# Last stage of a fused attention and two-layer kernel: each tile's eight transposes made together in two row halves, and the splits of the weight sums regrouped by inner block

## The chip, the core and the metric

The kernel runs on one core of a Trainium2 chip. The metric is the device time of one execution in microseconds (us). Smaller is better. TensorE (PE) multiplies and transposes; its weight loads are listed apart as PEld. VectorE (DVE), ScalarE (ACT) and GpSimd (POOL) do the elementwise work, and SyncE (SP) issues the DMAs. Every engine runs its own instructions in the order in which they stand.

## The reference

A causal attention, and behind it two feed-forward layers, the second with a SoLU and a layer normalisation between its two products. The change lies in the very last product, `ln @ w_out`, and in what feeds it.

```python
attn_out = causal_softmax(q @ k.T / 8) @ v        # 2 x 12 heads, 448 x 64
x = attn_out, heads side by side                  # 896 tokens x 768
h = x @ moe_w_in                                  # 768 x 2048
x = (h * sigmoid(h)) @ moe_w_out                  # 2048 x 768
h = x @ moe2_w_in                                 # 768 x 1024
e = np.exp(h - h_max)
sm = e / (np.sum(e, axis=-1, keepdims=True) + 1e-09)
solu = h * sm
mu = np.mean(solu, axis=-1, keepdims=True)
var = np.mean((solu - mu) ** 2, axis=-1, keepdims=True)
ln = (solu - mu) / np.sqrt(var + 1e-06) * g_ln
return (ln @ moe2_w_out).astype(np.float32)       # 1024 x 768
```

Products run in a reduced float32 format, so each operand is split into a high and a low part, and a product is three matmuls: high by high, high by low, low by high.

## The kernel before

The kernel goes through stages: attention, first layer up, first layer down, then the second layer. In the second layer the 896 tokens are seven tiles t = 0 to 6 of 128 rows. `gemm3(t)` (L647 to L649) makes the 128 x 1024 block of h in one of two tiles of the PSUM pool `psh` (two banks each). `chain(t)` turns it into ln: a maximum on DVE (L661), Exp on ACT (L662), scaling on DVE (L664 to L667), a Square on ACT that writes back into the `psh` tile (L669), and Identity on ACT (L670). The result stands in SBUF as `es4[t]`, eight blocks of 128 columns.

For the last product ln must be transposed. `turn(t, n)` (L680) transposes half a tile, four blocks of 128 x 128, into one bank of the pool `pst`, which has two buffers of one bank. `take(t, n)` then makes the two parts: ACT copies the bank into the high part (L684), DVE subtracts that from the bank into the low part (L685). `take` of both halves is the step `takes` for tile 1 and `take(0, 1)`, `take(0, 2)` for tile 0.

Tiles 0, 1 and 2 are multiplied plainly: `whole(t, n)` makes 24 matmuls for each half of the columns (`product`, L703 to L705) in one bank, and ACT scales the result to SBUF (L729). Tiles 3 to 6 go in two pairs by a Strassen-like scheme, `pair4(g)`: seven products of 12 matmuls, named after their operands ("11", "12", "s4", "s2", "s3", "s1", "22"), on sums of the transposed halves (made by `pre(g, n)`: L845, L691, L684, L685) and on weights or sums of weight blocks. DVE adds the results up (L743). The weight sums are made in place by `sums4(k)` for each inner block k = 0 to 3 (ACT scales four blocks, L825; POOL adds, L827 to L830). `split_t(z)` splits a weight sum t1 to t4 into parts, one copy on ACT (L836) and one subtraction on DVE (L837) for each k.

The order is written out by hand. `after()` is called behind each product, and the table `steps` says which of these preparations stand behind which call: call 0 and 1 belong to `whole(0, 0)`, 2 and 3 to `whole(0, 1)`, and so on to 11; calls 12 to 18 belong to `pair4(1)` and 19 to 25 to `pair4(2)`. `whole(0, 0)` itself is called inside `chain(6)`, between the scaling and the Square. In PSUM the seven tiles leave this division: two banks `gm` for the products, two `pst`, four `psh`; `psh` is given back behind `whole(2, 1)`, and `psq` (two banks for products) takes part of its place.

Of the kernel before, what the change touches and what calls it, by code (L numbers as in the profile page):

```python
# [80 lines left out]
def fused(ctx, tc, qk, vv, w1, w2, w3, w4, gl, out):  # L81
# [34 lines left out]
    with tc.manual_schedule():  # L116
# [514 lines left out]
        psd.release()  # L631
        pst = pool("pst", 2, space=PS)
        psh = pool("psh", 2, space=PS)
# [42 lines left out]

        def turn(t, n):
            tp = tps[t, n] = pst.tile([128, K2, 128], F32, name="tp", tag="tp")
            for m in range(K2):
                nc.tensor.transpose(tp[:, m], half(t, n - 1)[:, m], ident)  # L680

        def parts(z, x, low):
            h, l = aop[z]
            nc.scalar.activation(h, x, AF.Copy)  # L684
            low.tensor_tensor(l, x, h.bitcast(F32), ALU.subtract)  # L685

        def take(t, n, z=None):
            parts(z or (t, n), tps.pop((t, n)) if z is None else tps[t, n], nc.vector)

# [93 lines left out]
        for t in range(NT):  # L783
            gemm3(t)
            if t == 0:
                fill()
            if t == NT - 2:
                turn(0, 1)
                turn(0, 2)

            def first():
                if t == NT - 2:
                    take(0, 1)
                    take(0, 2)
                fill()

            if t < NT - 1:
                chain(t, first, fill)
# [10 lines left out]
        def arrive(t):  # L809
            turn(t, 1)  # L810
            turn(t, 2)
            take(t, 1)
            take(t, 2)
# [17 lines left out]

        def split_t(z, ks=range(K2)):
            q = {"t1": "11", "t2": "22", "t3": "12", "t4": "21"}[z]
            h, l = split[4, z]
            for k in ks:
                nc.scalar.activation(h[:, k], quads[q, k], AF.Copy)  # L836
                nc.vector.tensor_tensor(l[:, k], quads[q, k], h[:, k].bitcast(F32), ALU.subtract)  # L837

        def pre(g, n):
            a, b = 2 * g + 1, 2 * g + 2  # L840
            s1, s3, s2, s4 = half(b, 1), half(b, 0), half(a, 0), half(a, 1)
            if n == 0:
                turn(b, 1)
                turn(b, 2)
                nc.scalar.activation(s3, tps[b, 1], AF.Copy)  # L845
                add(s1, tps[b, 2], s3, ALU.add)
                take(b, 2, (g, "22"))
            elif n == 1:
                turn(a, 1)
                take(a, 1, (g, "11"))  # L850
                add(s2, s1, tps[a, 1], ALU.subtract)
                add(s3, s3, tps[a, 1], ALU.subtract)
            elif n == 2:
                turn(a, 2)
                take(a, 2, (g, "12"))
                add(s4, tps[a, 2], s2, ALU.subtract)
                parts((g, "s4"), s4, nc.gpsimd)
            else:
                z = ("s2", "s3", "s1")[n - 3]
                parts((g, z), {"s1": s1, "s2": s2, "s3": s3}[z], nc.gpsimd)  # L860

        steps = {1: [lambda: sums4(1)], 3: [lambda: sums4(2)], 4: [lambda: arrive(2)], 5: [lambda: sums4(3)],
                 6: [lambda: pre(1, 0)], 7: [lambda: pre(1, 1)], 8: [lambda: split_t("t2", (0, 1))],
                 9: [lambda: pre(1, 2)], 10: [lambda: split_t("t2", (2, 3))], 11: [lambda: pre(1, 3), lambda: split_t("t3")],
                 12: [lambda: split_t("t1"), lambda: pre(1, 4)], 13: [lambda: split_t("t4"), lambda: pre(1, 5)],
                 14: [lambda: pre(2, 0)], 15: [lambda: pre(2, 1)], 16: [lambda: pre(2, 2)],
# [11 lines left out]
        sums4(0)  # L878
        turn(1, 1)
        turn(1, 2)  # L880
        chain(NT - 1, takes, lambda: whole(0, 0))
        whole(0, 1)
        for t in (1, 2):
            for n in range(2):
                whole(t, n)
        psh.release()
        banks[0] = pool("psq", 2, space=PS)
        for g in (1, 2):
            pair4(g)
        banks = [q for q in banks if q is not gm]  # L890
        banks[0].release()
        pst.release()
# [54 lines left out]
```

## Time and profile before

| | |
|---|---|
| Median of three runs | 408.0 us (407.79 to 408.76) |
| The profiled execution, its own time | 408.79 us |
| Its span, first to last instruction | 407.0 us |
| PE busy in the span | 398.4 us (98%) |
| Chain of work that ended last, by engine | PE 85%, DVE 9%, ACT 4%, issue 1% |

How to read it: the profile lists one execution, each instruction with start and duration in us from the span's start. In a timeline, the brackets at a row's end give the engine's idle time just before it and the instruction whose end released it. Matmuls overlap: each starts when its predecessor is about half done. The share of busy time is a mean over stages; what counts for this change is the stretch from 335 us to the end.

### The profile page before, as it was taken

The page shows a single profiled execution, that of the slowest core. Times are in us where ns is not written, and L with a number is a line of the kernel's source. Part 1 is how long each engine was busy: PE and PEld are TensorE (multiplying, and loading weights), DVE is VectorE, ACT ScalarE, POOL GpSimd, SP SyncE. Part 2 cuts the span into 40 slices and gives each one's busy share as a digit, 9 for nine tenths or more (in the row PEclk, how much of TensorE's full clock was granted, in tenths as well). Part 3 has the DMA queues.
Part 4 walks back from the last instruction along what each step waited for, and adds up shares of the span by engine and source line. Part 5 has one row for each costly group of instructions (what it writes and reads, how often), then busy time and mean ns, then how long its engine had stood idle before and what let it go on. Part 6 is the DMA issues. An engine that isn't in the chain of part 4 may idle for free.

```text
span 407.0 us, 7456 instructions
## 1 busy us (share of the span) xinstructions
PE 398.4 (98%) x2593; PEld 370.2 (91%) x2593; DVE 346.7 (85%) x739; ACT 239.6 (59%) x551; POOL 206.8 (51%) x222
## 2 busy tenths in 40 slices
PE   8899999999999999999999999999999999999896
PEld 6677777899999999999999999999988889999796
DVE  4999999799999999998898979857999997537953
ACT  4999999543535353535544445444657785996530
POOL 2998773377777777775454433335500000792240
PEclk9999999999999999999999999999999999999999
DMA  7775322134434343434765757655023310021021
GB/s 252 245 261 170 119 85 79 40 98 136 129 106 126 106 131 103 129 105 124 235 201 182 229 168 229 184 159 155 2 82 114 115 40 2 19 60 39 21 78 59
DMA packets 19798, 50.03 MB, mean 123 GB/s; under 512 B 2352, under 2 KB 4528, under 8 KB 19760
## 3 DMA queue, kind: packets, MB, share of 16 engines
q1 hardware_dynamic: 19760, 49.56, 39.6%
q8 instruction: 20, 0.33, 0.3%
q14 instruction: 18, 0.15, 0.1%
HBM read 46.80 MB, written 2.75 MB: 122 GB/s over the span
## 4 chain that ended last, share of the span: by engine, by line
PE 85%; DVE 9%; ACT 4%; issue 1%; DVEq 0%; SPq 0%
PE h L382 8%; PE h L381 8%; PE h L380 8%; PE h L508 7%; PE h L510 7%; PE h L509 7%; PE x L258 5%; PE h L649 4%; PE h L648 4%; PE h L647 4%; PE x L168 3%; PE x L232 3%; DVE e L198 3%; PE ps L705 2%; PE ps L703 2%; PE ps L704 2%
## 5 line engine op out<-in xcount | busy, mean ns | idle before, releaser
L316 POOL TENSOR_TENSOR wl<-wx,wh 128x384 fp32r<-128x384 f32 x64 | 83.1, 1301 | 72.3 <-ACT wh L312 48.8
L285 ACT ACTIVATE wr<-wr 128x384 f32<-128x384 f32 x96 | 56.9, 596 | 33.6 <-DMA wr<-w_in 33.4
L296 DVE SCALAR_TENSOR_TENSOR wx<-wr,wx 128x384 uint32<-128x384 uint32 x96 | 70.1, 730 | 0.1
L312 ACT ACTIVATE wh<-wx 128x384 fp32r<-128x384 f32 x64 | 33.2, 520 | 58.2 <-DVE wx L296 33.0
L290 DVE SCALAR_TENSOR_TENSOR wx<-wr 128x384 uint32<-128x384 uint32 x96 | 60.9, 634 | 2.2 <-POOL gl L391 1.3
L381 PE MATMUL h<-x,wh 128*128 128x448 f32 x174 | 61.3, 352 | 0.0
L380 PE MATMUL h<-x,wh 128*128 128x448 f32 x174 | 61.3, 352 | 0.0
L382 PE MATMUL h<-x,wl 128*128 128x448 f32 x174 | 61.3, 352 | 0.0
L306 DVE TENSOR_SCALAR wr<-wr 128x384 uint32<-128x384 uint32 x96 | 57.7, 602 | 3.2 <-DMA wr<-w_in 3.1
L509 PE MATMUL h<-gl,wh 128*128 128x448 f32 x160 | 56.4, 352 | 0.0
L508 PE MATMUL h<-gh,wh 128*128 128x448 f32 x160 | 56.4, 352 | 0.0
L510 PE MATMUL h<-gh,wl 128*128 128x448 f32 x160 | 56.4, 352 | 0.0
L218 POOL TENSOR_TENSOR e<-e,st 128x128 f32<-128x128 f32 (+3 forms) x70 | 44.0, 664 | 20.3 <-DVE st L211 15.3
L391 POOL TENSOR_TENSOR gl<-sg,gh 128x448 fp32r<-128x448 f32 x32 | 40.6, 1268 | 16.5 <-DVE gh L390 8.9
L204 ACT ACTIVATE e<-e,st 128x128 f32<-128x128 f32 (+3 forms) x84 | 43.9, 540 | 4.4 <-DVE st L198 4.4
L198 DVE CUSTOM_DVE_ANT_0 e<-x,mask 128x128 f32<-128x128 f32 (+3 forms) x84 | 32.9, 445 | 5.3 <-PE x L168 5.3
L380 PEld LDWEIGHTS h<-x,wh 128*128 128x128 f32 x174 | 32.9, 189 | 0.1
L382 PEld LDWEIGHTS h<-x,wl 128*128 128x128 f32 x174 | 32.9, 189 | 0.0
L381 PEld LDWEIGHTS h<-x,wh 128*128 128x128 f32 x174 | 32.9, 189 | 0.0
L647 PE MATMUL h<-w3h,y 128*128 128x512 f32 x84 | 31.9, 380 | 0.0
L648 PE MATMUL h<-w3l,y 128*128 128x512 f32 x84 | 31.8, 379 | 0.0
L649 PE MATMUL h<-w3h,y 128*128 128x512 f32 x84 | 31.8, 379 | 0.0
(204 smaller groups left out, 871.2 us busy)
## 6 DMA issues: line engine op xcount, KB each, us to landing
wr<-w_in SPq DMA_DIRECT2D x96, 384.0 KB, 3.5
qk<-qk_in SPq DMA_DIRECT2D x11, 480.0 KB, 5.1
v<-vv_in SPq DMA_DIRECT2D x12, 256.0 KB, 4.8
out<-o SPq DMA_DIRECT2D x12, 192.0 KB, 1.9
out<-o SPq DMA_DIRECT2D x4, 96.0 KB, 2.2
qk<-qk_in SPq DMA_DIRECT2D x2, 128.0 KB, 2.4
qk<-qk_in SPq DMA_DIRECT2D x1, 224.0 KB, 2.8
gain<-gl_in SPq DMA_DIRECT2D x1, 4.0 KB, 3.6
```

Source lines behind the costliest of these rows:

```text
L285: nc.scalar.activation(high, high, AF.Copy, scale=DOWN)
L290: nc.vector.scalar_tensor_tensor(x.bitcast(U32), r[:, :, 1], 0x80000000, r[:, :, 0], ALU.bitwise_and, ALU.bitwise_or)
L296: nc.vector.scalar_tensor_tensor(xu, r[:, :, 1], 3, xu, ALU.logical_shift_left, ALU.bitwise_or)
L306: nc.vector.tensor_scalar(low, low, 29, None, ALU.logical_shift_right)
L316: eng.tensor_tensor(l, wx.pop((n, c)), h.bitcast(F32), ALU.subtract)
L380: nc.tensor.matmul(ps[:, :S], wh, rh, start=turn == 0 and k % NB == 0, stop=False)
L381: nc.tensor.matmul(ps[:, :S], wh, rl, start=False, stop=False)
L382: nc.tensor.matmul(ps[:, :S], wl, rh, start=False, stop=turn == 1 and k % NB == NB - 1)
L508: nc.tensor.matmul(ps[:, :S], wh, rh, start=f == 0, stop=False)
L509: nc.tensor.matmul(ps[:, :S], wh, rl, start=False, stop=False)
L510: nc.tensor.matmul(ps[:, :S], wl, rh, start=False, stop=f == KF - 1)
L647: nc.tensor.matmul(ps[:, n], yh[:, k, at], wh, start=k == 0, stop=False)
```

## The change

Three things change in the last stage.

1. `turn(t)` makes all eight transposes of a tile at once, each as two transposes of 64 rows: the upper row half of a block goes to one bank, the lower to the other. A tile of transposes now fills two banks, and every bank holds row halves of all eight blocks. The pool `pst` has one buffer of two banks. `take` and `pre` read each half of the blocks out of both banks, and write the operands in the old layout through the view `rows`.
2. A second such buffer, the pool `pstb`, is opened behind `chain(6)` in the place of `psh`, which is given back there instead of behind `whole(2, 1)`. `psq` is opened at the same point. From then on the two buffers take turns, `pstb` first. `arrive(2)` moves from call 4 to call 3, `pre(1, 0)` from call 6 to 5; `pre(1, 2)` has no transposes of its own any more, nor has `pre(2, 2)`.
3. `split_t(k)` splits the four weight sums of one inner block k; it stands one or more calls behind the `sums4(k)` that makes them: at calls 2, 8, 10 and 11 instead of by weight sum at calls 8 to 13.

```diff
-        pst = pool("pst", 2, space=PS)
+        pst = pool("pst", 1, space=PS)
@@
-        def turn(t, n):
-            tp = tps[t, n] = pst.tile([128, K2, 128], F32, name="tp", tag="tp")
-            for m in range(K2):
-                nc.tensor.transpose(tp[:, m], half(t, n - 1)[:, m], ident)
+        turns = [pst]
+
+        def rows(a):
+            return a.rearrange("p k (z q) -> p k z q", q=C)
+
+        def turn(t):
+            turns.append(turns.pop(0))
+            tp = turns[-1].tile([128, 2, 512], F32, name="tp", tag="tp")
+            for m in range(KF2):
+                for z in range(2):
+                    r = slice(C * z, C * z + C)
+                    nc.tensor.transpose(tp[:, z, C * m:C * m + C], es4[t][r, m], ident[r, r])
+            both = tp.rearrange("p z (m q) -> p m z q", q=C)
+            tps[t, 1], tps[t, 2] = both[:, :K2], both[:, K2:]
@@
-        def split_t(z, ks=range(K2)):
-            q = {"t1": "11", "t2": "22", "t3": "12", "t4": "21"}[z]
-            h, l = split[4, z]
-            for k in ks:
+        def split_t(k):
+            for z, q in (("t2", "22"), ("t3", "12"), ("t1", "11"), ("t4", "21")):
+                h, l = split[4, z]
                 nc.scalar.activation(h[:, k], quads[q, k], AF.Copy)
                 nc.vector.tensor_tensor(l[:, k], quads[q, k], h[:, k].bitcast(F32), ALU.subtract)
@@
             if n == 0:
-                turn(b, 1)
-                turn(b, 2)
+                turn(b)
...
             elif n == 1:
-                turn(a, 1)
+                turn(a)
...
             elif n == 2:
-                turn(a, 2)
@@
-        steps = {1: [lambda: sums4(1)], 3: [lambda: sums4(2)], 4: [lambda: arrive(2)], 5: [lambda: sums4(3)],
-                 6: [lambda: pre(1, 0)], 7: [lambda: pre(1, 1)], 8: [lambda: split_t("t2", (0, 1))],
-                 9: [lambda: pre(1, 2)], 10: [lambda: split_t("t2", (2, 3))], 11: [lambda: pre(1, 3), lambda: split_t("t3")],
-                 12: [lambda: split_t("t1"), lambda: pre(1, 4)], 13: [lambda: split_t("t4"), lambda: pre(1, 5)],
+        steps = {1: [lambda: sums4(1)], 2: [lambda: split_t(0)], 3: [lambda: arrive(2)], 4: [lambda: sums4(2)],
+                 5: [lambda: pre(1, 0)], 6: [lambda: sums4(3)], 7: [lambda: pre(1, 1)], 8: [lambda: split_t(1)],
+                 9: [lambda: pre(1, 2)], 10: [lambda: split_t(2)], 11: [lambda: split_t(3), lambda: pre(1, 3)],
+                 12: [lambda: pre(1, 4)], 13: [lambda: pre(1, 5)],
...
         chain(NT - 1, takes, lambda: whole(0, 0))
+        psh.release()
+        psq = pool("psq", 2, space=PS)
+        turns.insert(0, pool("pstb", 1, space=PS))
         whole(0, 1)
         for t in (1, 2):
             for n in range(2):
                 whole(t, n)
-        psh.release()
-        banks[0] = pool("psq", 2, space=PS)
+        banks[0] = psq
```

Two places of the order show what moves. The first is PE around the transposes of tile 2 (`arrive(2)`). Before, they stand inside `whole(1, 0)`, the second half of them behind a wait for DVE:

```order
L705 MATMUL ps<-b11h,area 128x384
L680 MATMUL tp<-ident,e 128x128 [waits PE_49]
L680 MATMUL tp<-ident,e 128x128 x3
L680 MATMUL tp<-ident,e 128x128 [waits DVE_49]
L680 MATMUL tp<-ident,e 128x128 x3
L703 MATMUL ps<-b21h,area 128x384
```

Now, with the numbers of lines in the changed file (L688 transposes, L713 to L715 products), they stand ahead of `whole(1, 0)`, in the last products of `whole(0, 1)`:

```order
L713 MATMUL ps<-b22h,d_3526 128x384 [waits Activation_49]
L714 MATMUL ps<-b22l,d_3526 128x384 [waits DVE_49]
L715 MATMUL ps<-b22h,d_3527 128x384
L688 MATMUL tp<-ident,e 128x64 [waits PE_49,Activation_49]
L688 MATMUL tp<-ident,e 128x64 x15
L713 MATMUL ps<-b11h,area 128x384
```

The transposes have moved 12 matmuls forward, and their first one waits for ACT: its tile is the first in `pstb`, whose banks held the h of tile 6, and the last ACT instruction on that h is the Square of `chain(6)`.

The second place is ACT from the Exp of `chain(6)` on. Before (L684 is the copy of `take`, L729 the scaling of a product of `whole`, L825 that of `sums4`):

```order
L662 ACTIVATE e,s<-h,s 128x1024 [waits DVE_49]
L684 ACTIVATE area<-tp 128x512 [waits PE_49] x2
L729 ACTIVATE o<-ps,s 128x384 [waits PE_49,Pool_49]
L825 ACTIVATE wx<-wx,gain 128x384 x4
L669 ACTIVATE h,s<-e,s 128x1024 [waits DVE_49]
L670 ACTIVATE e<-e,s 128x1024 [waits Activation_49]
L729 ACTIVATE o<-ps,s 128x384 [waits PE_49]
```

Now (L694, L739 and L833 are the same three instructions, L843 the copy of `split_t`):

```order
L662 ACTIVATE e,s<-h,s 128x1024 [waits DVE_49]
L694 ACTIVATE area<-tp 128x512 [waits PE_49]
L694 ACTIVATE area<-tp 128x512 [waits DVE_49]
L739 ACTIVATE o<-ps,s 128x384 [waits PE_49,Pool_49]
L833 ACTIVATE wx<-wx,gain 128x384 x4
L669 ACTIVATE h,s<-e,s 128x1024 [waits DVE_49]
L670 ACTIVATE e<-e,s 128x1024 [waits Activation_49]
L843 ACTIVATE t2h<-wx 128x384 [waits Pool_49]
L843 ACTIVATE t3h<-wx 128x384
L843 ACTIVATE t1h<-wx 128x384
L843 ACTIVATE t4h<-wx 128x384 [waits Pool_49]
L739 ACTIVATE o<-ps,s 128x384 [waits PE_49]
```

The second copy of a `take` pair now waits for DVE, where it waited for PE alone, and four copies of `split_t(0)` stand behind `chain(6)`, ahead of the scaling of `whole(0, 1)`.

## Rows read from the trace of the kernel before

**Rows 1.** The page: busy time by engine, then the granted clock in 40 slices.

```profile
PE 398.4 (98%) x2593; PEld 370.2 (91%) x2593; DVE 346.7 (85%) x739; ACT 239.6 (59%) x551; POOL 206.8 (51%) x222
PEclk9999999999999999999999999999999999999999
```

**Rows 2.** Timeline of PE, last stage: start, duration, line, operation, shape, count, idle.

```profile
335.62 1.04 PE L680 MATMUL tp<-ident,e 128*128 128x128 f32 x8
336.42 0.46 PE L647 MATMUL h<-w3h,y 128*128 128x512 f32 x1
...
352.94 0.33 PE L703 MATMUL ps<-b11h,area 128*128 128x384 f32 x1
...
359.51 0.33 PE L705 MATMUL ps<-b12h,area 128*128 128x384 f32 x1
360.35 1.25 PE L680 MATMUL tp<-ident,e 128*128 128x128 f32 x8 [0.51 <-DVE area L685]
361.36 0.41 PE L703 MATMUL ps<-b22h,area 128*128 128x384 f32 x1
...
383.13 0.33 PE L705 MATMUL ps<-t3h,area 128*128 128x384 f32 x1
385.11 0.63 PE L680 MATMUL tp<-ident,e 128*128 128x128 f32 x4 [1.65 <-DVE area L685]
385.49 0.41 PE L703 MATMUL ps<-t1h,area 128*128 128x384 f32 x1
```

**Rows 3.** Timeline of PE in attention: a group of 32 row-half transposes, what follows.

```profile
65.97 1.32 PE L232 MATMUL x<-ident,e 64*128 64x64 f32 x32
67.22 3.68 PE L258 MATMUL x<-aT,v 128*64 128x448 f32 x32
```

**Rows 4.** Instructions on the tile tp: duration in ns, smallest/median/largest, first and last start.

```profile
L684 ACT ACTIVATE area<-tp x9: 580/593/599, 350.4 to 385.8; 128x512 fp32r<-128x512 f32 x9
L685 DVE TENSOR_TENSOR area<-tp,area x9: 681/691/692, 351.1 to 388.2; 128x512 fp32r<-128x512 f32 x9
```

**Rows 5.** Timelines of DVE and ACT, chains of tiles 5 and 6, and a split.

```profile
338.81 1.29 DVE L685 TENSOR_TENSOR d<-tp,d 128x512 fp32r<-128x512 f32 x2 [1.76 <-ACT d L684]
343.99 1.12 ACT L669 ACTIVATE h<-e,s 128x1024 f32<-128x1024 f32 x1 [3.11 <-DVE s L667]
350.45 1.06 ACT L684 ACTIVATE area<-tp 128x512 fp32r<-128x512 f32 x2
351.06 1.29 DVE L685 TENSOR_TENSOR area<-tp,area 128x512 fp32r<-128x512 f32 x2 [1.82 <-ACT area L684]
354.16 1.12 ACT L669 ACTIVATE h<-e,s 128x1024 f32<-128x1024 f32 x1 [0.15 <-DVE s L667]
355.21 0.19 ACT L669 ACTIVATION_READ_ACCUMULATOR h<-e,s 128x1 f32 x1
355.43 1.15 ACT L670 ACTIVATE e<-e,s 128x1024 f32<-128x1024 f32 x1
373.28 1.75 ACT L836 ACTIVATE t3h<-wx 128x384 fp32r<-128x384 f32 x4
```

**Rows 6.** Busy time by engine and granted clock (the number ahead of DMA's two).

```profile
403.00:404.00 1.00, 0.29 (x2) 0.00 (x0) 0.62 (x1) 0.00 (x0) 0.00 (x0) 1.00 0.97 346
405.00:406.00 1.00, 0.00 (x0) 0.00 (x0) 0.00 (x0) 0.00 (x0) 0.00 (x0) 1.00 0.37 134
406.00:407.00 1.00, 0.00 (x0) 0.00 (x0) 0.00 (x0) 0.00 (x0) 0.00 (x0) 0.69 0.00 0
```

**Rows 7.** Timeline of PE at the program's start.

```profile
1.39 2.23 PE L398 MATMUL x<-x 128*128 128x448 f32 x5 [1.39 <-DVE x L393]
...
5.42 1.95 PE L178 MATMUL x<-qk 64*128 64x224 f32 x8
7.21 1.46 PE L168 MATMUL x<-qk 64*128 64x256 f32 x12
8.51 1.30 PE L178 MATMUL x<-qk 64*128 64x224 f32 x12
```

More of the change, by code (lines that the diff above doesn't have):

```diff
@@ L675, in fused @@
         tps = {}
-        def turn(t, n):
-            tp = tps[t, n] = pst.tile([128, K2, 128], F32, name="tp", tag="tp")
-            for m in range(K2):
-                nc.tensor.transpose(tp[:, m], half(t, n - 1)[:, m], ident)
+        turns = [pst]
[10 more added lines that the diff above has]
+            tps[t, 1], tps[t, 2] = both[:, :K2], both[:, K2:]
         def parts(z, x, low):
-            h, l = aop[z]
+            h, l = [rows(a) for a in aop[z]]
             nc.scalar.activation(h, x, AF.Copy)
@@ L687, in take @@
         def take(t, n, z=None):
-            parts(z or (t, n), tps.pop((t, n)) if z is None else tps[t, n], nc.vector)
+            parts(z or (t, n), tps[t, n], nc.vector)
         def add(o, a, b, op):
@@ L787, in fused @@
             if t == NT - 2:
-                turn(0, 1)
-                turn(0, 2)
+                turn(0)
             def first():
@@ L809, in arrive @@
         def arrive(t):
-            turn(t, 1)
-            turn(t, 2)
+            turn(t)
             take(t, 1)
@@ L840, in pre @@
             a, b = 2 * g + 1, 2 * g + 2
-            s1, s3, s2, s4 = half(b, 1), half(b, 0), half(a, 0), half(a, 1)
+            s1, s3, s2, s4 = [rows(half(*at)) for at in ((b, 1), (b, 0), (a, 0), (a, 1))]
             if n == 0:
-                turn(b, 1)
-                turn(b, 2)
+                turn(b)
                 nc.scalar.activation(s3, tps[b, 1], AF.Copy)
@@ L878, in fused @@
         sums4(0)
-        turn(1, 1)
-        turn(1, 2)
+        turn(1)
         chain(NT - 1, takes, lambda: whole(0, 0))
+        psh.release()
+        psq = pool("psq", 2, space=PS)
+        turns.insert(0, pool("pstb", 1, space=PS))
         whole(0, 1)
@@ L885, in fused @@
                 whole(t, n)
-        psh.release()
-        banks[0] = pool("psq", 2, space=PS)
+        banks[0] = psq
         for g in (1, 2):
             pair4(g)
-        banks = [q for q in banks if q is not gm]
-        banks[0].release()
+        turns.remove(pst)
+        turns[0].release()
+        psq.release()
         pst.release()
```

## The prediction

> **What bounds the kernel now.** I read the page's busy times first: PE is busy 98% of the span [rows 1], and in the stretch that the change touches, from 335 us to the end, it runs without a pause but for two. So what counts is what PE itself executes and where it waits. The timeline of PE shows both [rows 2]. Seven tiles of transposes stand between the matmuls. Two groups wait for DVE to empty a one-bank buffer: at 360.35 and at 385.11. A product's matmuls start 0.16 apart (each lasts 0.33 and overlaps the next by half), so PE could have gone on at 359.51 + 0.16 = 359.67 and at 383.13 + 0.16 = 383.29. The two waits are worth 0.68 and 1.82 us. Then I read ACT and DVE around 338 to 357 us [rows 5], since the order puts a new wait on ACT there.
>
> The sum is made against the profiled execution: 408.79 us with a span of 407.0. The median of the runs, 408.0, is 0.8 below it; I carry the difference over to the median. A measurement of this kernel tells about 0.3% from no change, 1.2 us, so the lines are 406.8 and 409.2.
>
> **The change part by part.**
>
> *Transposes.* Before, a group of eight takes 336.42 - 335.62 = 0.80 us until the next matmul starts, and three more groups are like it. The group at 360.35 takes 1.01, since its second half waits too, and there are four groups of four of about 385.49 - 385.11 = 0.38 [rows 2]. Together 4 x 0.80 + 1.01 + 4 x 0.38 = 5.73 us. After, there are seven groups of 16 transposes of 64 rows. Attention has the same instruction, also with the two row halves in two banks: 32 of them take 67.22 - 65.97 = 1.25 us, 0.039 each [rows 3]. So a tile takes 0.62, seven take 4.37, and 1.36 us are saved. The bounds: at 0.80 a tile nothing but the 0.13 of smaller groups is saved; if the halves ran wholly side by side, 0.31 a tile, 3.56 would be. I take the row of the same instruction.
>
> *The two waits.* `pre(1, 0)` now writes into `pst`, whose last reader is the `take` of tile 1, done at 351.06 + 1.29 = 352.35 [rows 5], long before. In `pre(2, 1)` the buffer `pstb` was last read by `pre(1, 2)`. Both waits go: 2.50 us. Before, the second one hung on DVE's subtractions of t4, which stood ahead of the `take` on its queue; these now stand earlier, and the transposes don't ask for them.
>
> *The new wait.* `arrive(2)` is moved ahead of `whole(1, 0)`, and its buffer is the first in `pstb`. The order shows that its first transpose waits for ACT: for the Square of `chain(6)`, which uses the banks that `psh` gives back. Before, that Square starts at 354.16 and ends, with the reading of its accumulator, at 355.21 + 0.19 = 355.40 [rows 5]. PE reaches the place at 352.94 in the trace [rows 2], earlier by 2 x 0.18 for the two tiles of transposes ahead of it: 352.58. Even with an unchanged Square, PE stands still for 2.8 us, with all products of `whole(1, 0)` and what follows queued behind the transposes.
>
> The Square also comes later. In a `take` pair the second copy now waits for the first subtraction, as the order shows. A copy takes 0.59 and a subtraction 0.69 [rows 4]; the hop between them is 0.02 (350.45 + 0.59 = 351.04, DVE starts at 351.06). From the first subtraction to the end of the second one it is now 0.69 + 0.02 + 0.59 + 0.02 + 0.69 = 2.01 instead of 1.29: 0.72 more [rows 5]. The pair of tile 0 (338.81) is followed on DVE by the rest of `chain(5)`, for whose result ACT waits with its Square at 343.99 (3.11 idle), and from there ACT works through to the copies at 350.45. So these come 0.72 later. The pair of tile 1 (351.06) stands ahead of the scaling of `chain(6)`, for which the Square at 354.16 waits: another 0.72. The Square is done at 355.40 + 1.44 = 356.84, and PE stands still from 352.58 to 356.86, 4.28 us.
>
> The trace of before shows the second copy running beside the first subtraction, two copies in 1.06 us and DVE's first subtraction between them [rows 5]; there the halves lie in two banks. The Trainium skill (PSUM — Partial Sum Buffer, section "PSUM bank collisions raise a hardware error") says that two engines must not touch one bank in the same quadrant of partitions at the same time, reads against reads included. By that rule the wait can't go while both halves share both banks, and the sum stands; if the reads could overlap, the standstill would be 2.84 us and the time 407.0.
>
> *The splits.* They are as many as before, 16 copies on ACT and 16 subtractions on DVE, only moved. Four copies, 1.75 us [rows 5], now stand behind the Identity of `chain(6)` and ahead of the scaling of `whole(0, 1)`, which frees the bank of `whole(1, 1)`. Identity starts at 355.43 + 1.44 = 356.87 and takes 1.15, so the scaling starts at 359.8. PE, restarted at 356.86, needs the bank 0.62 + 24 x 0.16 = 4.5 us later, at 361.3. A scaling takes about as long as a copy, 0.6, so 0.9 us of slack cover the move: 0, and if the cover is gone some 0.7, the size of the smaller wait of before. They also free DVE of its backlog at 378 to 382. I take 0.
>
> *Sum without the clock:* -1.36 - 2.50 + 4.28 = +0.42, so 408.4 us.
>
> *The clock.* PE has not stood still for 4 us anywhere in the program before. Where it stops for good, the trace shows what the clock does: PE's last matmul ends at 403.29, the granted clock is 1.00 in 405 to 406 and 0.69 on average in 406 to 407 [rows 6]. Between the levels 1.00 (2.4 GHz) and 0.50 (1.2 GHz) that is a fall at 406.4, 3.1 us after the last matmul. In the wait of 1.82 us it stays in the nines [rows 1]. The new standstill is longer than 3.1 us, so I expect PE to restart at 1.2 GHz. What that costs is bounded by the program's start: PE begins at 1.39, and eight matmuls of 64x224 take 1.95 us at 5.42 (0.24 each) but twelve take 1.30 at 8.51 (0.11 each); the 64x256 at 7.21 are already fast [rows 7]. So PE ran at half rate for up to 5.8 us after its first work, whatever the granted clock's row prints for it. At half rate half of that time is lost: between 0 and 2.9 us. Both ends are far from sure, as PE is fed more densely here than at the start; I take the middle, 1.45.
>
> The Trainium skill (TensorE: Matmul & The Clock Gate, section "Why this matters for your kernels") warns of idle gaps of PE between bursts of matmuls, which put the clock back to half. No row here shows such a gap inside the program; by the rule the time is 409.9, without it 408.4.
>
> **Forecast:** 408.0 + 0.42 + 1.45 = 409.9 us, slower by 0.5%.
>
> **The rivals.**
>
> *The clock stays (not slower).* The place is the standstill at 352.6 to 356.9. If the granted clock is still 1.00 when PE restarts, nothing but the sum counts: 408.4, no change that can be told. For it speaks that only one row shows a fall, at the end of the program, and that 4.28 us is not far beyond 3.1; it decides as soon as the standstill is near 3 us.
>
> *A shorter wait.* If the `take` pairs don't delay the Square, the standstill is 2.84 us and the clock has no cause to fall: 408.0 - 3.86 + 2.84 = 407.0, no change. Against it stand the waits that the order shows on ACT.
>
> *Cheaper transposes.* At 0.31 a tile a further 2.2 us go, and with the clock up that is 406.2, faster. Against it: attention's row halves go to two banks already, and take 0.039 [rows 3].
>
> **How the numbers follow.** Forecast 0.47, the clock stays 0.35, a shorter wait 0.10, cheaper transposes 0.06; 0.02 are left for other stalls that make it slower. Of the second case some 0.05 lies over 409.2, by the 0.7 of the splits, and of the forecast some 0.02 under it, where the low level lasts for less than 1.6 us. So slower is 0.47 - 0.02 + 0.05 + 0.02 = 0.52, same 0.41, faster 0.07. The range goes from the shorter wait, 407.0, to the forecast with the clock's upper bound, 408.4 + 2.9 = 411.3; the forecast's own range is 408.4 to 411.3.
>
> **What would show it.** In the timeline of PE after: no idle time for DVE ahead of the transposes, 0.62 for a tile, and one idle stretch of about 4.3 us ahead of the transposes of tile 2, ended by ACT's Square. In ACT's timeline the second copy of each `take` starts 0.7 later than the first one's end. In the windows behind 356 us a granted clock under 1.00, and product matmuls 0.33 apart instead of 0.16. The forecast is wrong if that idle stretch is under 3 us, or if the clock reads 1.00 right behind it.

## The result, and the profile after

The changed kernel takes 410.98 us (median of four runs, 410.46 to 411.10) where the kernel before took 407.89 on the same chip: a ratio of 1.0069, 95% interval 1.0051 to 1.0086. It is 0.7% slower. The profiled execution took 410.46 us, with a span of 408.7. The page of after, busy time of PE and granted clock, against [rows 1]:

```profile
PE 398.1 (97%) x2649; PEld 369.5 (90%) x2649; DVE 348.0 (85%) x739; ACT 239.6 (59%) x551; POOL 203.8 (50%) x222
PEclk9999999999999999999999999999999999989999
```

PE has 56 more instructions (transposes of half the rows) and is busy for 0.3 us less. One slice of the clock's row shows an eight where before all showed nines. The view of waits for PE, from 318 us on, has one line (tile and line, releaser: us in total, times, longest):

```profile
PE tp L688 <- ACT h L669: 3.9, 1, 3.9
```

Both waits for DVE of [rows 2] are gone, and one wait for ACT's Square has come. PE's timeline shows the place, and what follows it (start, duration, line, operation, shape, count, idle and its releaser):

```profile
351.92 0.33 PE L715 MATMUL ps<-b22h,d 128*128 128x384 f32 x1
356.19 0.96 PE L688 MATMUL tp<-ident,e 64*128 64x64 f32 x16 [3.94 <-ACT h L669]
357.08 0.69 PE L713 MATMUL ps<-b11h,area 128*128 128x384 f32 x1
357.56 0.53 PE L714 MATMUL ps<-b11l,area 128*128 128x384 f32 x1
...
359.48 0.51 PE L714 MATMUL ps<-b11l,area 128*128 128x384 f32 x1
359.80 0.36 PE L715 MATMUL ps<-b11h,area 128*128 128x384 f32 x1
...
362.27 0.33 PE L715 MATMUL ps<-b21h,area 128*128 128x384 f32 x1
362.52 0.71 PE L688 MATMUL tp<-ident,e 64*128 64x64 f32 x16
363.17 0.43 PE L713 MATMUL ps<-b12h,area 128*128 128x384 f32 x1
363.44 0.33 PE L714 MATMUL ps<-b12l,area 128*128 128x384 f32 x1
```

PE could have gone on at 351.92 + 0.16 = 352.08 and does so at 356.19: it stands still for 4.11 us. From 357.56 to 359.80 its matmuls start 0.32 apart, twice the usual 0.16. The windows by microsecond give the clock (the number ahead of the DMA's two; busy time of PE, PEld, DVE, ACT and POOL stand ahead of it):

```profile
355.00:356.00 1.00, 0.00 (x0) 0.00 (x0) 0.00 (x0) 1.00 (x2) 0.99 (x1) 1.00 0.16 34
356.00:357.00 1.00, 0.81 (x16) 0.78 (x16) 0.15 (x1) 0.97 (x3) 0.93 (x1) 0.72 0.00 0
357.00:358.00 1.00, 1.00 (x7) 0.92 (x4) 0.24 (x1) 1.00 (x3) 0.92 (x2) 0.50 0.02 8
358.00:359.00 1.00, 1.00 (x5) 1.00 (x4) 1.00 (x3) 1.00 (x4) 0.98 (x2) 0.50 0.00 0
359.00:360.00 1.00, 1.00 (x6) 1.00 (x5) 1.00 (x4) 0.93 (x2) 0.00 (x0) 0.57 0.00 0
360.00:361.00 1.00, 1.00 (x8) 1.00 (x8) 0.65 (x1) 0.32 (x1) 0.00 (x0) 1.00 0.42 89
```

The clock goes from 2.4 to 1.2 GHz at about 356.4 and back at about 359.9. Why the Square is late stands in the timelines of ACT and DVE, against [rows 5]:

```profile
350.43 0.58 ACT L694 ACTIVATE area<-tp 128x512 fp32r<-128x512 f32 x1
351.77 0.60 ACT L694 ACTIVATE area<-tp 128x512 fp32r<-128x512 f32 x1 [0.76 <-DVE area L695]
354.89 1.12 ACT L669 ACTIVATE h<-e,s 128x1024 f32<-128x1024 f32 x1
355.95 0.19 ACT L669 ACTIVATION_READ_ACCUMULATOR h<-e,s 128x1 f32 x1
```

The second copy of the `take` pair starts 1.34 behind the first, when DVE's subtraction of the first half is done. Before, the two ran as one stretch of 1.06.

From the first transposes of the stage to PE's last matmul the kernel before took 402.96 - 335.62 = 67.34 us, and the changed one 404.63 - 334.92 = 69.71, 2.37 more. The ends of these stretches, the first line from the kernel before:

```profile
402.96 0.33 PE L705 MATMUL ps<-t4h,area 128*128 128x384 f32 x1
334.92 0.71 PE L688 MATMUL tp<-ident,e 64*128 64x64 f32 x16
404.63 0.33 PE L715 MATMUL ps<-t4h,area 128*128 128x384 f32 x1
```

It adds up so. The transposes, counted from the last matmul ahead of a group to the second one behind it, less the matmuls' own pace, cost 6.53 before and 5.80 after: -0.73. (What the waits, the standstill and the low clock add to a group is left out of this and counted below.) The two waits: -2.50. The standstill: +4.11. The low clock: the transposes of tile 2 take 0.89 until the next matmul instead of 0.65, and the gaps behind them are 1.34 over those of another tile: +1.58. The sum is +2.46. That is 0.09 more than 2.37, since the sum counts the border ahead of the first group too, which lies ahead of the stretch. The medians differ by 3.1 us, and the interval of the ratio means 2.1 to 3.5 us; what the 3.1 has beyond the rows is in no row here. Ahead of the stage the executions differ by themselves: in the profiled ones of all kernels here, which are alike up to that point, it starts between 334.8 and 335.9.

### The profile page after: what moved, and what is told of

Its sections match the earlier page's. It is cut to its first block, busy times and chain, and to the rows that moved or that the text cites. A ratio compares the mean times of both kernels' runs of the same rounds, so it can differ in the third digit from the quotient of the medians.

```text
span 408.7 us, 7567 instructions
## 1 busy us (share of the span) xinstructions
PE 398.1 (97%) x2649; PEld 369.5 (90%) x2649; DVE 348.0 (85%) x739; ACT 239.6 (59%) x551; POOL 203.8 (50%) x222
## 4 chain that ended last, share of the span: by engine, by line
PE 88%; DVE 6%; ACT 3%; DMA 1%; issue 0%; SPq 0%; DVEq 0%
PE h L382 8%; PE h L381 8%; PE h L380 8%; PE h L508 7%; PE h L510 7%; PE h L509 7%; PE x L258 5%; PE ps L713 4%; PE h L649 4%; PE h L648 4%; PE h L647 4%; PE ps L714 4%; PE ps L715 4%; DVE e L198 3%; PE x L232 3%; PE x L168 2%
## 5 line engine op out<-in xcount | busy, mean ns | idle before, releaser
L316 POOL TENSOR_TENSOR wl<-wx,wh 128x384 fp32r<-128x384 f32 x64 | 80.1, 1255 | 75.4 <-ACT wh L312 55.6
```

The source lines that it names most:

```text
L316: eng.tensor_tensor(l, wx.pop((n, c)), h.bitcast(F32), ALU.subtract)
```

## The experiments

My theory: the standstill on the Square (made by the choice of the buffer and by copies that wait for subtractions in shared banks), and the fall of the clock behind it, are the whole loss. The rivals: ACT's and DVE's queues are too full with the moved splits, so that the time would be lost in any case; or the row halves themselves are dear. The kernel before was timed beside each. Its median was 408.3 to 408.6 on these chips, some 0.5 above that of the first result, so ratios are compared and not microseconds.

| kernel | us | ratio to before | 95% interval |
| --- | --- | --- | --- |
| changed, once more | 411.06 | 1.0069 | 1.0052 to 1.0087 |
| changed, PE kept busy in the standstill | 409.60 | 1.0026 | 1.0015 to 1.0038 |
| changed, `arrive(2)` one call later | 408.93 | 1.0010 | 1.0001 to 1.0018 |
| changed, `pst` ahead of `pstb` | 408.79 | 1.0007 | 0.9995 to 1.0019 |
| changed, 128-row transposes, a bank for each half | 408.28 | 1.0009 | 0.9991 to 1.0026 |
| the same, PE kept busy in the standstill | 408.20 | 0.9998 | 0.9985 to 1.0011 |
| changed, 128-row transposes, halves share both banks | 411.16 | 1.0066 | 1.0052 to 1.0079 |
| changed, 128-row transposes, a bank for each half, `pst` first | 406.17 | 0.9945 | 0.9933 to 0.9957 |
| before + regrouped splits | 408.28 | 0.9997 | 0.9988 to 1.0005 |
| before + second buffer, `pst` first | 405.74 | 0.9927 | 0.9915 to 0.9939 |
| the last + row halves | 407.78 | 0.9981 | 0.9972 to 0.9990 |

### Is it the idle time that brings the clock down?

Twenty matmuls are added ahead of the transposes of tile 2:

```diff
-            o, ps = outs[t][n], bank()
+            o, ps = outs[t][n], ahead.pop() if ahead else bank()
...
         def arrive(t):
+            ahead.append(bank())
+            for _ in range(20):
+                nc.tensor.matmul(ahead[0], split[4, "11"][0][:, 0, :128], split[4, "11"][0][:, 0], start=True, stop=True)
             turn(t)
```

> 20 matmuls of 128x384 are added ahead of the transposes of tile 2, into the bank that the first product of whole(1, 0) takes and overwrites next: work added, nothing left out. They fill about 3.2 us (20 x 0.16) of the 4.11 us that PE stands still there; the wait for the Square of chain(6) itself stays. Theory 'clock': PE's half rate behind the wait (about 1.6 us) comes from its having been idle for 4.1 us. Then the transposes still start near 356.2, their product matmuls come 0.16 apart at once, the granted clock stays near 1.00 behind 356 us, and the time is 411.0 - 1.6 = 409.4. Rival 'mode': the half rate behind the wait is not from the idle time (it comes from the row-half transposes at that place). Then the matmuls are still 0.32 apart and the time stays at 411.0.

Measured: 1.0026. PE's timeline of this kernel, and the end of ACT's Square in it:

```profile
352.26 0.33 PE L715 MATMUL ps<-b22h,d 128*128 128x384 f32 x1
353.21 3.76 PE L821 MATMUL ps<-b11h 128*128 128x384 f32 x20 [0.62 <-ACT o L739]
356.90 0.71 PE L688 MATMUL tp<-ident,e 64*128 64x64 f32 x16
357.54 0.43 PE L713 MATMUL ps<-b11h,area 128*128 128x384 f32 x1
357.80 0.33 PE L714 MATMUL ps<-b11l,area 128*128 128x384 f32 x1
356.27 0.19 ACT L669 ACTIVATION_READ_ACCUMULATOR h<-e,s 128x1 f32 x1
```

One of its windows, with the columns as above:

```profile
357.00:358.00 1.00, 1.00 (x19) 0.93 (x20) 0.00 (x0) 1.00 (x3) 0.92 (x2) 1.00 0.03 8
```

The place is the same, the transposes are no earlier, the matmuls come 0.16 apart at once and the clock reads 1.00. All six executions show a clock of 0.998 or more. The fall comes from the idle time. I had expected the transposes near 356.2; they start at 356.90. Half of that is the stage's later start in this execution (335.27 against 334.92), the rest is made by the added matmuls, which started 0.8 late, behind a wait for their bank, and end behind the Square. The difference of the ratios, 0.0043, is 1.8 us, and the two intervals leave it open by some 0.9 us either way; the rows behind the standstill give 1.58.

### How surely does it fall?

> The changed kernel once more, unaltered, on the same chip as the three that follow, to see how often the clock falls behind its standstill of 4.1 us. With row halves undone (standstill 2.3 us) it fell in 5 of 12 executions, and each fall cost 2.4 us. Theory 'length': a standstill of 4.1 us brings the fall in every execution: all granted clocks near 0.995, times within 1 us of each other, 0.7% over the kernel before. Rival 'chance': the fall doesn't depend on the length, and some 4 in 10 executions fall: then the times lie in two groups some 1.6 us apart.

Measured: 1.0069 again, and all six granted clocks are 0.991 to 0.996, as were the four of the first result. After 4.1 us of standstill the clock fell in ten executions of ten. That is "length", but for the times: they spread from 410.17 to 412.44, not within 1 us. Of the two above 412 one shows a clock of 0.991, the other 0.995, and no trace here shows what they lost. The next pair shows a shorter one. The changed kernel gets back the transposes of 128 rows, with a bank for each half of a tile:

```diff
-        pst = pool("pst", 1, space=PS)
+        pst = pool("pst", 2, space=PS)
...
-            tp = turns[-1].tile([128, 2, 512], F32, name="tp", tag="tp")
-            for m in range(KF2):
-                for z in range(2):
-                    r = slice(C * z, C * z + C)
-                    nc.tensor.transpose(tp[:, z, C * m:C * m + C], es4[t][r, m], ident[r, r])
+            for n in (1, 2):
+                tp = turns[-1].tile([128, K2, 128], F32, name="tp", tag="tp")
+                for m in range(K2):
+                    nc.tensor.transpose(tp[:, m], half(t, n - 1)[:, m], ident)
+                tps[t, n] = rows(tp)
...
-        turns.insert(0, pool("pstb", 1, space=PS))
+        turns.insert(0, pool("pstb", 2, space=PS))
```

> The row halves alone are undone: a tile's transposes are eight of 128 rows in two groups of four, each with a one-bank tile of its own (two in pst, two in pstb), as before; the order of the steps, the splits and the two places of buffers stay as in the changed kernel. Theory 'lock': the second copy of a take then runs beside the first subtraction, each take is 0.72 shorter, the Square of chain(6) comes up to 1.44 earlier and the idle stretch ahead of the transposes of tile 2 is 4.11 - 1.44 = 2.7 (at most 3.4), the clock stays or falls for less; 7 x 0.05 more for the transposes than the measured 0.83 a tile: 411.0 - 1.4 - 1.6 + 0.4 = 408.4. Rival 'cheap halves': the row halves are worth the 1.36 us that I had forecast, and the lock costs nothing since ACT would be late anyway: 411.0 + 1.4 = 412.4.

Measured: 1.0009, but in two groups. Seven executions took 407.5 to 408.4 us with a clock of 0.998 to 1.000, five took 410.3 to 410.5 with 0.994. The profiled one is of the second group. PE's timeline in it:

```profile
352.97 0.33 PE L713 MATMUL ps<-b22h,d 128*128 128x384 f32 x1
355.61 1.97 PE L687 MATMUL tp<-ident,e 128*128 128x128 f32 x8 [2.31 <-ACT h L669]
357.23 0.67 PE L711 MATMUL ps<-b11h,area 128*128 128x384 f32 x1
```

ACT's timeline around the copies and the Square:

```profile
350.61 1.06 ACT L692 ACTIVATE area<-tp 128x512 fp32r<-128x512 f32 x2
354.31 1.12 ACT L669 ACTIVATE h<-e,s 128x1024 f32<-128x1024 f32 x1 [0.16 <-DVE s L667]
```

Two windows around the restart:

```profile
355.00:356.00 1.00, 0.39 (x2) 0.39 (x3) 0.15 (x1) 0.97 (x3) 0.92 (x2) 0.78 0.00 0
356.00:357.00 1.00, 1.00 (x7) 1.00 (x6) 0.00 (x0) 1.00 (x2) 0.92 (x2) 0.50 0.03 8
```

The two copies run as one stretch of 1.06 again, and PE stands still for 355.61 - 353.13 = 2.48 us instead of 4.11. That is "lock" as expected. I had expected the clock to stay up, since it fell 3.1 us behind the last matmul at the end of the program [rows 6]. It fell in five of the twelve executions, in the profiled one at 355.56. So 3.1 us is no limit below which the clock is safe. With ten added matmuls in this kernel's standstill:

```diff
+            ahead.append(bank())
+            for _ in range(10):
+                nc.tensor.matmul(ahead[0], split[4, "11"][0][:, 0, :128], split[4, "11"][0][:, 0], start=True, stop=True)
```

> The kernel with row halves undone (a bank for each half; standstill 2.3 us, times in two groups, 5 executions at 410.3 to 410.5 with a granted clock of 0.994 and 7 at 407.5 to 408.4 with 0.998 to 1.000) with 10 matmuls of 128x384 added ahead of the transposes of tile 2, into the bank that whole(1, 0) takes and overwrites next: work added, nothing left out. They fill 1.6 us of the 2.3; the wait for the Square stays. Theory 'clock': the two groups differ by the fall alone. Then no execution shows a clock under 0.998, all times lie in the lower group, about 0.1% under before, and the transposes start at the same time against the Square as without the added matmuls. Rival 'two speeds of the rest': the two groups have another cause (the Square's date, say), and the clock only follows: then there are still two groups, some 2 us apart.

Measured: 0.9998. All eleven granted clocks are 0.998 to 1.000. Ten times lie between 407.4 and 408.8; the eleventh, 410.33 at a clock of 1.000, has a cause that no trace here shows. PE's timeline in its profiled execution:

```profile
352.49 1.90 PE L819 MATMUL ps<-b11h 128*128 128x384 f32 x10
354.99 1.09 PE L687 MATMUL tp<-ident,e 128*128 128x128 f32 x8 [0.59 <-ACT h L669]
355.83 0.41 PE L711 MATMUL ps<-b11h,area 128*128 128x384 f32 x1
```

The window behind them:

```profile
356.00:357.00 1.00, 1.00 (x8) 1.00 (x7) 0.44 (x1) 1.00 (x4) 1.00 (x2) 1.00 0.00 0
```

From the place where PE could have gone on with its work, 352.49, to the transposes it is 2.50 us, as without the added matmuls. From the first transposes to the last matmul this execution is 1.60 us shorter than the profiled one with the fall (335.17 to 402.16 against 335.81 to 404.40). The two executions differ by 2.27 us in all; 0.64 of that lies ahead of the stage, and I haven't settled what it goes with.

### Would the time have been lost in any case?

Two small edits of the changed kernel take PE off the Square. In one, `arrive(2)` goes back to call 4:

```diff
-        steps = {1: [lambda: sums4(1)], 2: [lambda: split_t(0)], 3: [lambda: arrive(2)], 4: [lambda: sums4(2)],
+        steps = {1: [lambda: sums4(1)], 2: [lambda: split_t(0)], 4: [lambda: arrive(2), lambda: sums4(2)],
```

> arrive(2) goes back one call, to call 4 ahead of sums4(2); all else as in the changed kernel. Half of whole(1, 0)'s matmuls, 1.95 us, come ahead of the wait for the Square. Theory 'standstill': the wait is a fixed date, so the idle stretch shrinks by 1.95 to about 2.2 us, under the 3.1 after which a fall was seen; the clock stays, 1.6 + 1.95 = 3.5 us would go, 407.5, if nothing else came to be late; by the rows of ACT and DVE its copies of tile 2 come later too and some 0.5 to 1 us return as waits for banks behind it: 408.0. Rival 'queue': what was lost is the longer work on ACT and DVE (the splits moved ahead, the copies behind the subtractions), the wait on PE is only where it shows, and the idle time comes back in full further on: only the clock's 1.6 us go, 409.4.

In the other, the buffers take turns from `pst` on:

```diff
-        turns.insert(0, pool("pstb", 1, space=PS))
+        turns.append(pool("pstb", 1, space=PS))
```

> The two buffers of the transposes change turns: tile 2 goes into pst, which is free early, and tile 4 into pstb, which stands where the banks of psh were. All else as in the changed kernel. Theory 'standstill': the wait on the Square at the transposes of tile 2 goes; they wait for the subtractions of tile 1 instead, about 1.1 us, the clock stays; 4.11 - 1.1 + 1.6 = 4.6 us would go, 406.4, with the rest of ACT's backlog some 1 to 1.5 us of it return as waits for banks: 407.9. Rival 'queue': ACT and DVE set the pace here, and nearly all of the standstill returns as PE's waits on ACT and DVE behind it: 409.4, the clock's part alone.

Measured: 1.0010 and 1.0007. All eleven clocks of the first are 0.998 or more, and eleven of the twelve of the second (one execution, 410.77 us, has 0.996). PE's waits in the first:

```profile
PE tp L688 <- ACT h L669: 1.1, 1, 1.1
PE ps L715 <- POOL area L695: 0.8, 1, 0.8
PE ps L713 <- ACT o L739: 0.6, 1, 0.6
```

Both come out within 0.3 us of what the theory gave (its 408.0 and 407.9 are ratios of 1.0003 and 1.0000 to the 407.9 of before), far from the rival's 1.004. But the theory had a part of the rival in it: in the first, 2.5 us in all stay or return as waits for ACT and POOL. So the choice of the buffer, by the standstill and the clock together, cost 0.0062, 2.5 us. Repairing it brings the kernel back to the time before, and no further.

### Which part is worth what?

The second buffer alone, on the kernel before: `psq` and `pstb` are opened ahead of `whole(0, 1)`, the two places take turns, `pst` first, with 128-row transposes and two one-bank tiles each; steps and splits stay. Since a place now holds a whole tile, the eight transposes of a tile stand together in `pair4` too, where before there were groups of four.

```diff
...
+            turns.append(turns.pop(0))
+            for n in (1, 2):
+                tp = turns[-1].tile([128, K2, 128], F32, name="tp", tag="tp")
...
+        psh.release()
+        psq = pool("psq", 2, space=PS)
+        turns.append(pool("pstb", 2, space=PS))
         whole(0, 1)
...
```

> The kernel before with the second pair of banks for the transposes alone: psq and pstb are opened ahead of whole(0, 1), the two places take turns tile by tile, two one-bank tiles each, pst first; transposes of 128 rows, the steps and the splits as before (arrive(2) at call 4, t4's splits at call 13). Theory 'buffers': both waits of before (0.68 and 1.82 us) go, no transposes wait for the Square of chain(6) for long since tile 2 goes to pst, and tile 4, which goes into the new place, comes 9 us later; the smaller gap between groups of four saves 0.1: 2.5 us faster than before, 0.6%. Rival 'queues': DVE's subtractions of t4 and ACT's backlog hold up the products instead, and less than 1 us is gained: not told from before.

Measured: 0.9927, 2.6 us under the kernel of before beside it. The view of waits has no line for PE from 318 us on. PE's rows around tile 2, where the changed kernel stood still:

```profile
354.46 0.33 PE L713 MATMUL ps<-b11h,area 128*128 128x384 f32 x1
354.62 1.04 PE L687 MATMUL tp<-ident,e 128*128 128x128 f32 x8
355.42 0.41 PE L711 MATMUL ps<-b21h,area 128*128 128x384 f32 x1
355.66 0.33 PE L712 MATMUL ps<-b21l,area 128*128 128x384 f32 x1
```

That is the fastest kernel of this study, and faster than both. Row halves added to it, as in the changed kernel:

```diff
-        pst = pool("pst", 2, space=PS)
+        pst = pool("pst", 1, space=PS)
...
-            for n in (1, 2):
-                tp = turns[-1].tile([128, K2, 128], F32, name="tp", tag="tp")
...
+            tp = turns[-1].tile([128, 2, 512], F32, name="tp", tag="tp")
+            for m in range(KF2):
+                for z in range(2):
+                    r = slice(C * z, C * z + C)
+                    nc.tensor.transpose(tp[:, z, C * m:C * m + C], es4[t][r, m], ident[r, r])
...
-        turns.append(pool("pstb", 2, space=PS))
+        turns.append(pool("pstb", 1, space=PS))
```

> The second pair of banks alone (0.73% faster than before, no wait of PE from 330 us on) with the transposes in row halves into two banks as in the changed kernel, and nothing else: here no transposes stand behind the Square, so what the row halves do by themselves is seen. Theory 'lock': the transposes save 0.05 us a tile, 0.35 in all, but each pair of copies is 0.72 longer on ACT and DVE, PE has to wait for ACT and DVE ahead of whole(1, 0) and whole(1, 1) and in the first products of pair4(2), about 3 us in all: 2 to 2.7 us slower than the second pair of banks alone, not told from before. Rival 'cheap halves': copies and subtractions have slack enough without the standstill, PE still waits nowhere, and it is 0.35 to 1.3 us faster than the second pair of banks alone, 0.8 to 1.0% faster than before.

Measured: 0.9981. Against 0.9927 that is 0.0054, 2.2 us lost (the two medians differ by 2.04). The waits that come back in it, as the view of waits lists them:

```profile
PE ps L713 <- ACT o L739: 0.6, 1, 0.6
PE ps L715 <- POOL area L695: 0.3, 1, 0.3
```

They are only part of it: in its timeline PE also starts single matmuls late by 0.1 to 0.3 near 358.6 and from 388 to 393 us, some 2.4 us in all with the two listed. The transposes give back 0.25. Is it the halves, or the banks that they share? In the changed kernel, with transposes of 128 rows but each half of a tile spread over both banks:

```diff
-            return a.rearrange("p k (z q) -> p k z q", q=C)
+            return a.rearrange("p (b j) q -> p b j q", j=2)
...
+            for n in (1, 2):
+                for m in range(K2):
+                    c = 256 * (n - 1) + 128 * (m % 2)
+                    nc.tensor.transpose(tp[:, m // 2, c:c + 128], half(t, n - 1)[:, m], ident)
+                tps[t, n] = tp[:, :, 256 * (n - 1):256 * n].rearrange("p b (j q) -> p b j q", j=2)
```

> The changed kernel with transposes of 128 rows, but with each half of a tile's output spread over both banks, so that the second copy still has to wait for the first subtraction. Against the changed kernel it lacks the row halves alone; against the kernel with row halves undone and a bank for each half it has the lock alone. Theory 'lock': the take pairs take as long as in the changed kernel, the standstill ahead of the transposes of tile 2 is 3.9 to 4.1 us again, the clock falls in every execution, and the transposes cost 0.35 more: 0.75% slower than before, about 411.4. Rival 'row halves': what lengthens the pairs is reading the outputs of the row halves, not the shared banks: the standstill is 2.3 us as without row halves, the clock falls in some executions, and the time is that of that kernel, 0.1% over before in the middle.

Measured: 1.0066, all six clocks 0.991 to 0.995. ACT's timeline at the copies of tile 1:

```profile
350.34 0.58 ACT L693 ACTIVATE area<-tp 128x512 fp32r<-128x512 f32 x1
351.68 0.60 ACT L693 ACTIVATE area<-tp 128x512 fp32r<-128x512 f32 x1 [0.76 <-DVE area L694]
```

PE's transposes of tile 2:

```profile
356.10 1.77 PE L688 MATMUL tp<-ident,e 128*128 128x128 f32 x8 [3.84 <-ACT h L669]
```

The idle 0.76 of ACT is there without any row half, and PE stands still for 4.00 us. So the layout over both banks makes the lock, and not the row halves. What in the layout does it stays open: the wait is one that the program itself has (the order in "The change" shows it), and wherever the halves share banks here, they also lie in one tile of the pool, while a bank for each half also meant a tile for each. One tile of two banks with a bank for each half was not run. The time can't be told from that of the changed kernel: the row halves in themselves gain nothing that can be measured. By PE's timelines they are worth some 0.25 us: seven groups of 128 rows at 0.80 and 0.08 behind each, against 0.645 and 0.20 at the borders.

The regrouped splits alone, on the kernel before:

```diff
-        def split_t(z, ks=range(K2)):
...
+        def split_t(k):
+            for z, q in (("t2", "22"), ("t3", "12"), ("t1", "11"), ("t4", "21")):
...
+        steps = {1: [lambda: sums4(1)], 2: [lambda: split_t(0)], 3: [lambda: sums4(2)], 4: [lambda: arrive(2)], 5: [lambda: sums4(3)],
+                 6: [lambda: pre(1, 0)], 7: [lambda: pre(1, 1)], 8: [lambda: split_t(1)],
+                 9: [lambda: pre(1, 2)], 10: [lambda: split_t(2)], 11: [lambda: split_t(3), lambda: pre(1, 3)],
```

> The kernel before with the third part of the change alone: the splits of the weight sums by inner block, at calls 2, 8, 10 and 11 instead of 8 and 10 to 13; the full transposes, the two one-bank buffers and all other steps as before. My forecast took the splits at 0, with 0.7 if their cover is gone. Theory 'backlog moved': the wait of 1.82 us at the transposes behind DVE's subtractions of t4 goes, but the four copies of the first block stand ahead of scalings on ACT and a wait for ACT of about 1 us, and a longer wait for DVE at the transposes of tile 4 (0.7 -> 1.3), come instead: -1.8 + 1.0 + 0.6 = -0.2, no change that can be told from before. Rival 'splits free': the 1.8 us go and nothing comes back: 0.45% faster than before. Rival 'splits cost': the wait of 1.8 us goes over to another place and the new ones are added: 0.3% slower.

Measured: 0.9997, and these waits of PE:

```profile
PE tp L680 <- DVE area L685: 1.0, 1, 1.0
PE ps L703 <- ACT o L729: 0.9, 1, 0.9
```

The wait of 1.65 idle at 385.11 [rows 2] is gone, the one at 360.35 has grown from 0.51 to 1.0, and one of 0.9 for ACT's scaling has come. That is "backlog moved". Last, the changed kernel with both faults mended, 128-row transposes with a bank for each half (the diff above) and `pst` first:

```diff
-        turns.insert(0, pool("pstb", 1, space=PS))
+        turns.append(pool("pstb", 2, space=PS))
```

> The changed kernel with two things put back or turned: transposes of 128 rows in two one-bank tiles, and pst ahead of pstb, so that tile 2 doesn't wait for the Square. The steps and the splits stay as in the changed kernel. Against the kernel of the second pair of banks alone it has the third part of the change more. Theory 'two faults': the change is hurt by the wait on the Square and by the copies locked behind the subtractions; without both, what is left are a wait of 0.2 us for ACT and about 0.6 us for POOL's s2: 1.7 to 2 us faster than before, 0.4 to 0.5%, and some 0.7 us behind the second pair of banks alone. Rival 'steps': the new order of the steps is at fault by itself: at least 1 us of waits on ACT stay ahead of whole(1, 0) and whole(1, 1), and it is not told from before.

Measured: 0.9945, with one wait of PE in the view of waits, 0.2 us for POOL. It is faster than before, and 0.0018, 0.7 us, behind the second buffer without the new steps and splits: the latter don't help on top of it. The intervals of the two, 0.9915 to 0.9939 and 0.9933 to 0.9957, overlap, so that the size of this last loss is not well fixed.

## Why the prediction was right, point by point

I forecast 409.9 us, 0.5% slower, by a standstill on the Square and a fall of the clock. It came out 0.7% slower, by just these two. By the rows it is +2.46 us where I had +1.87: the transposes were mis-sized by 0.63, the standstill by -0.17 and the clock by 0.13. What the medians have beyond that, some 0.6 us, is in no row.

*Transposes* (1.36 saved): mis-sized, 0.73 measured. The step priced a group from its first transpose to the next matmul, and that part was near: 0.65 a tile for 0.62. What I left out are the borders. A group of row halves starts 0.09 later behind a 128-row matmul than the next matmul would (362.27 to 362.52 is 0.25, not 0.16), and the second matmul behind it comes 0.27 after the first. Before, only the border behind a group cost something, 0.08 or 0.09. Attention's 32 in a row [rows 3] have no border inside them. The Trainium skill (TensorEngine Tiling (Array Packing), section "Key Properties") says that a change of the tiling mode drains TensorE; the 0.20 a group here agrees with it, and the prediction should have drawn on it. My own low bound for the saving was 0.13, and the rival of cheaper transposes stays out of reach.

*The two waits* (2.50 removed): right. Both are gone from the changed kernel, and the second buffer alone is worth 2.6. The second one goes by the regrouped splits alone as well, so the two parts don't add up there.

*The new wait* (4.28): right, 4.11. Both delays of 0.72 are in the trace. The second shows plainly: the Square starts at 354.89, 0.73 behind that of [rows 5]. The first was covered by the stage's starting 0.70 earlier in this execution; the Square of tile 5 is at 343.98 all the same, where [rows 5] have 343.99. With a bank for each half the standstill is 2.48, near the 2.84 of the rival of a shorter wait; with shared banks and no row halves it is 4.00. The rule of the Trainium skill that I weighed there (PSUM — Partial Sum Buffer, section "PSUM bank collisions raise a hardware error") fits the wait that the second copy shows, 0.76 us of idle time on ACT. But the wait stands in the program's order, and no run here tests the rule itself: whether the two reads would stand each other in one bank was not tried.

*The splits* (0): right in the sum, and in the changed kernel no wait for ACT's scaling is seen. But the slack of 0.9 us that I named was there only because PE had stood still for 4.1. Without a standstill the wait that I bounded at 0.7 is there: 0.9 with the splits alone, 0.6 with `arrive(2)` later.

*Sum without the clock* (+0.42, 408.4): with PE kept busy the ratio is 1.0026, +1.1 us on 408.5, 0.6 to 1.6 by its interval. Of that, some 0.4 is made by the added matmuls: the transposes start at 356.90, 0.44 behind the end of the Square at 356.46, and in the changed kernel 0.05 behind it. So +0.6 to +0.7, open by half a microsecond either way, stands against +0.42. The missing 0.63 of the transposes and the 0.17 less of the standstill give +0.88, which the measurement can't tell from either.

*The clock* (1.45): right that it falls, and 1.58 by the rows. That the middle of 0 to 2.9 came so near is partly luck. The slow matmuls of the program's start, from which I took the upper bound, stand where the clock's row prints nines [rows 1], and those just ahead of them were slow in another proportion:

```profile
3.55 2.08 PE L168 MATMUL x<-qk 64*128 64x128 f32 x8
```

These start 0.23 apart, as far as the 64x224 of [rows 7] with 0.24, for little more than half the columns. So a half rate alone doesn't explain that stretch, and it was no measure of the low clock; the 0.32 for 0.16 behind the standstill is one. The chance of 0.35 that it stays up was too high: it fell ten times in ten. The reason that I gave for the point of decision, 3.1 us from [rows 6], doesn't hold, since it also fell, five times in twelve, in a standstill of 2.5. The Trainium skill (TensorE: Matmul & The Clock Gate, section "Why this matters for your kernels") warned of such gaps, and the trace agrees: 0.50 of the clock behind a gap of 4.11 us.

What I didn't see is that the change has a good part. The buffer pays 2.6 us; what hides it are which of the two buffers comes first, and a layout in which two readers share one tile over the same banks.

## What to carry to other kernels

When a buffer is opened in the place of another one, look up whose last reader its first writer will wait for, and let the buffer that is free already be used first: one word here was worth 2.5 us. Two engines that read halves of one result in turn want the halves in tiles of their own, in different banks, as in the kernel before; with one tile over shared banks the second copy waited 0.76 us for the first subtraction, and the pair put 0.72 us on the path of whatever stood behind it on both queues. And a standstill of PE of some microseconds can cost more than its length: here 1.6 us on top of 4.1.

## What the runs showed of the hardware

- A group of 16 row-half transposes costs 0.20 us at its borders with 128-row matmuls, 0.09 ahead and 0.11 behind; a group of 128-row transposes 0.08 to 0.09, all of it behind.
- The clock's fall isn't tied to a fixed time after PE stops: about 356.4 in the changed kernel, 4.4 us after PE could have gone on and 0.2 behind its restart; 355.56 with the shorter standstill, 2.4 us after. In the changed kernel's second profiled execution it comes at about 357.3, when PE has been at work again for 0.9 us (the window 357 to 358 prints 0.66). With a standstill of 2.5 us it fell in five executions of twelve, with 4.0 to 4.1 in sixteen of sixteen, and with the gap filled but for some 0.8 us in none of seventeen. In the changed kernel with `pst` first, where no wait of the profiled execution is over 1.1 us, one of twelve shows 0.996; what happened in it no trace shows.
